# Six short loads behind the second MLP weight in a one-core decode kernel

## The chip, the core and the metric

The kernel runs on one core of a Trainium2 chip. The metric is the device time of one execution in microseconds; a kernel's time is the median of its runs. The profile that is shown comes from one execution taken by the hardware profiler; its span runs from the first to the last instruction.

## The reference, cut to what matters

One token passes through an attention branch and an MLP branch that share one normalized input. The results are added to the input.

```python
x = A_x                                   # [1, 1, 1024], bf16
xn = _layernorm(x)
return x + _A_ref(xn, k_cache, v_cache, wq, wo) + _B_ref(xn, w1, b1, w2, b2)

# attention: wq [1024, 4096], 32 query heads of 128, 4 key/value heads, last W = 4096 positions
q = (xn @ wq) ;  p = softmax(q k^T * 128**-0.5) ;  o = p v ;  return o @ wo        # wo [4096, 1024]
# MLP: w1 [1024, 3584], w2 [3584, 1024]
h = gelu(_layernorm(xn) @ w1 + b1) ;  return h @ w2 + b2
```

All weights and caches are bf16. With one token each weight is read once: wq 8.4 MB, w1 7.3 MB, w2 7.3 MB, wo 8.4 MB, and the used part of the caches 4.2 MB each, 39.85 MB together.

## The kernel before, in words

Every large operand is laid over the 128 partitions, so that each partition of a load is one contiguous run in memory (w1 and w2 are 56 KB per partition). All large loads are issued by SyncE (SP) into one DMA queue, in this order: the key cache in four loads (line 76), wq in two (line 85), w1 in one (line 200), the value cache in three (line 208), w2 in one (line 214), and wo in two halves, the first in one load and the second in five of shrinking size, 8, 4, 2, 1 and 1 rows of 1024 per partition (line 222). Four small loads go through ScalarE's queue at the start (lines 107 to 110): x as 32 partitions of 64 bytes, x and b2 as 4 partitions of 512 bytes each, b1 as 8 partitions of 896 bytes.

SP's loads are held back by the buffers that they fill. Large tiles share two slots of the pool `big` (the key cache and half of wq in one, the transposed keys in the other; later w1 takes the first and w2 the second), smaller ones two slots of `ring` (half of wq, the values, then the two halves of wo). So w1 waits until the first half of wq has been multiplied, w2 until the attention scores are done (line 260), and the second half of wo until the value product is done (line 296). The framework also gives each DMA one of eight completion semaphores in turn, and a load whose semaphore is still in use by the load eight places before it waits on SP for that load to land.

VectorE and ScalarE transpose the keys (lines 185 to 196). TensorE multiplies in the order wq (line 231), scores (260), w1 (243), values (296), w2 and wo (both line 323, into the accumulator `accf`; eight filler passes of line 321 stand between the two), and the last four rows of wo separately into `acct` (line 340). The last two steps, lines 344 and 345, add and cast the result, which goes out in two DMAs (lines 347 and 348).

The tile `w2t` has 32768 elements per partition. w2 fills 28672 of them (`CW2 * D`), the transposed activations `hT` (line 290) the next 896; the rest is unused. The list `chunk_src` holds the rows of w2 and wo that line 323 and line 340 go through.

Of the kernel before, what the change touches and what calls it, by code (L numbers as in the profile page):

```python
# [15 lines left out]
def kernel(  # L16
# [14 lines left out]
    nc = tc.nc  # L31
    P = 128
    D = A_x.shape[-1]
# [12 lines left out]
    CW2 = Fd // P  # L46
# [19 lines left out]
    def big_tile(name):  # L66
        return big.tile([P, 2 * RING_ELEMS], BF16, tag="big", name=name, align_bytes=256)
# [144 lines left out]
    w2t = big_tile("w2t")  # L212
    w2v = w2t[:, :CW2 * D].rearrange("p (r n) -> p r n", r=CW2)
    nc.sync.dma_start(out=w2v, in_=w2_v)
    chunk_src += [("h", r, w2v[:, r, :]) for r in range(CW2)]
    wo_v = A_wo.rearrange("(p c) n -> p c n", p=P)
    for i, cuts in enumerate([[0, 16], [0, 8, 12, 14, 15, 16]]):
# [8 lines left out]
    for i, w3 in enumerate(wq_tiles):  # L226
        for r in range(4):
            c = 4 * i + r
            for j in range(NJQ):
                b, t = divmod(j, 4)  # L230
# [148 lines left out]
```

## Time and profile before

| | us |
|---|---|
| median of three runs | 101.74 (101.66 to 102.03) |
| the profiled execution | 101.68 |
| its span | 100.0 |
| TensorE busy | 48.5 |
| VectorE busy | 38.2 |
| ScalarE busy | 29.2 |
| GpSimd busy | 8.6 |
| packets of SP's queue, share of 16 DMA engines over the span | 93.5% |
| moved, mean | 39.91 MB, 399 GB/s |

The time of the execution is 1.68 us above its span. Busy time of a compute engine is the time in which it executed; a share far below the span means that it waited for most of it. The DMA share is the busy time of the packets over 16 DMA engines. Besides the page's own views, the trace keeps a record of each DMA packet (queue, start, duration, size) and of each arrival at a completion semaphore; a load on all 16 DMA engines has 16 arrivals, one for each engine.

### The profile page before, as it was taken

Reading aid. Unit: us, or ns where it says so; the run is one execution under the profiler, and the core shown is the slowest. Engines: PE = TensorE matmul, PEld = TensorE weight load, DVE = VectorE, ACT = ScalarE, POOL = GpSimd, SP = SyncE. Lnnn points to the kernel's source line nnn. Section 1 sums busy time; section 2 is a strip of 40 time slices with the busy share of each in tenths; the row PEclk is TensorE's granted clock in tenths of the full one; section 3 lists DMA queues with packets and bytes.
Section 4 is the critical chain, followed back from the end, with each engine's and each line's share of the span. In section 5 each row is a group of like instructions: output and inputs, shape, how many; then the busy total and the mean of one; then the engine's idle time right before and its main releaser. Section 6 shows DMA issues by size and latency. Waiting matters only on the chain.

```text
span 100.0 us, 913 instructions
## 1 busy us (share of the span) xinstructions
PE 48.5 (49%) x361; PEld 19.5 (20%) x361; DVE 38.2 (38%) x26; ACT 29.2 (29%) x34; POOL 8.6 (9%) x33
## 2 busy tenths in 40 slices
PE   0006400008500940089149407997100999999980
PEld 0003100002100300053126203342000234224320
DVE  0069999999999970010631051002400000000020
ACT  5306100007999999900150440000400000000010
POOL 7911560000000000000001000000000000000000
PEclk9999999999995555555966997599755569999997
DMA  2999999999999888998599998998899999999910
GB/s 26 387 420 431 456 502 459 446 433 433 420 420 577 367 367 367 482 620 367 213 420 436 426 534 390 459 620 351 367 413 393 420 420 420 420 426 415 398 53 1
DMA packets 2663, 39.91 MB, mean 399 GB/s; under 512 B 338, under 2 KB 356, under 8 KB 740
## 3 DMA queue, kind: packets, MB, share of 16 engines
q1 hardware_dynamic: 2578, 39.85, 93.5%
q8 instruction: 3, 0.05, 0.2%
q10 hardware_dynamic: 82, 0.01, 0.1%
HBM read 39.86 MB, written 0.00 MB: 399 GB/s over the span
## 4 chain that ended last, share of the span: by engine, by line
DMA 80%; PE 14%; SPq 2%; issue 1%; DVE 0%
DMA v_sb<-in_A_v_cache_dram 33%; DMA wo<-in_A_wo_dram 25%; DMA kq<-in_A_wq_dram 17%; PE o_all L296 9%; DMA kq<-in_A_k_cache_dram 5%; PE accq L231 4%; SPq L222 1%; PE acct L340 1%; SPq L208 1%; DVE res L344 0%; PE acct L336 0%; SPq L200 0%
## 5 line engine op out<-in xcount | busy, mean ns | idle before, releaser
L194 ACT COPY kt<-kt 32x4096 bf16<-32x4096 bf16 x5 | 18.0, 3602 | 10.4 <-DVE kt L185 10.3
L185 DVE STREAM_TRANSPOSE kt<-kq 128x4096 bf16<-128x4096 bf16 x4 | 17.4, 4413 | 5.8 <-DMA kq<-in_A_k_cache_dram 5.8
L196 DVE COPY kt<-kt 32x4096 bf16<-32x4096 bf16 x11 | 13.4, 1219 | 0.2
L323 PE MATMUL accf<-w2t 128*1 128x512 bf16 x56 | 8.3, 466 | 5.7 <-DMA w2t<-in_B_w_dram 5.7
L296 PE MATMUL o_all<-v_sb,w1t 128*32 128x512 bf16 x32 | 8.8, 442 | 4.3 <-DMA v_sb<-in_A_v_cache_dram 4.3
L329 DVE COPY bulk<-accf 33x320 f32<-33x320 f32 x1 | 0.5, 482 | 24.7 <-ACT bulk L328 24.7
L231 PE MATMUL accq<-kq,xnT 128*1 128x512 bf16 x32 | 3.6, 627 | 10.2 <-DMA kq<-in_A_wq_dram 10.2
L323 PE MATMUL accf<-wo,o 128*1 128x512 bf16 x56 | 7.5, 378 | 0.1
L328 ACT COPY bulk<-accf 33x192 f32<-33x192 f32 x1 | 0.3, 312 | 23.2 <-PE accf L323 23.2
L231 PE MATMUL accq<-wq,xnT 128*1 128x512 bf16 x32 | 3.6, 626 | 6.1 <-DMA wq<-in_A_wq_dram 6.1
L231 PEld LDWEIGHTS <-xnT 128*1 128x1 bf16 x64 | 2.1, 116 | 20.5 <-issue 20.5
L296 PEld LDWEIGHTS <-w1t 128*32 128x32 bf16 x32 | 3.4, 109 | 9.6 <-DVE w2t L291 4.7
L323 PEld LDWEIGHTS <-w2t 128*1 128x1 bf16 x56 | 2.8, 98 | 10.8 <-issue 8.7
L243 PE MATMUL acch<-w1t,yT 128*1 128x448 bf16 x64 | 4.5, 450 | 0.0
L299 DVE TENSOR_TENSOR o_m<-o_all,grs 32x512 f32<-32x512 f32 x1 | 0.7, 678 | 9.0 <-PE o_all L296 9.0
L139 PE MATMUL x_ps<-x,zb 32*128 32x8 bf16 x4 | 0.2, 162 | 7.9 <-DMA x<-in_A_x_dram 7.9
L247 PE MATMUL qT_ps<-zb,w1t 128*128 128x128 bf16 x8 | 1.0, 311 | 6.2 <-ACT w1t L233 6.2
L303 ACT CAST o_bf<-o_f 32x128 bf16<-32x128 f32 x1 | 0.3, 297 | 12.5 <-DVE o_f L301 12.5
L291 DVE STREAM_TRANSPOSE w2t<-w1t 128x896 bf16<-128x896 bf16 x1 | 1.7, 1700 | 5.7 <-ACT w1t L288 5.7
L260 PE MATMUL sp<-kt,zb 128*32 128x512 bf16 x32 | 3.7, 631 | 0.3 <-DVE zb L252 0.3
L321 PE MATMUL spare<-zf,ident_f 128*1 128x512 f32 x8 | 3.6, 592 | 0.0
L323 PEld LDWEIGHTS <-o 128*1 128x1 bf16 x56 | 2.6, 82 | 4.3 <-issue 1.1
(78 smaller groups left out, 40.3 us busy)
## 6 DMA issues: line engine op xcount, KB each, us to landing
w1t<-in_B_w_dram SPq DMA_DIRECT2D x1, 7168.0 KB, 24.3
w2t<-in_B_w_dram SPq DMA_DIRECT2D x1, 7168.0 KB
kq<-in_A_k_cache_dram SPq DMA_DIRECT2D x4, 1024.0 KB, 8.1
kq<-in_A_wq_dram SPq DMA_DIRECT2D x1, 4096.0 KB, 17.1
wq<-in_A_wq_dram SPq DMA_DIRECT2D x1, 4096.0 KB, 24.1
wo<-in_A_wo_dram SPq DMA_DIRECT2D x1, 4096.0 KB
v_sb<-in_A_v_cache_dram SPq DMA_DIRECT2D x1, 2048.0 KB, 28.6
v_sb<-in_A_v_cache_dram SPq DMA_DIRECT2D x2, 1024.0 KB, 30.6
```

The source lines that it names most:

```text
L185: nc.vector.transpose(out=scr[:, g, :], in_=k2[:, g, :])
L194: nc.scalar.copy(out=dst, in_=src)
L196: nc.vector.tensor_copy(out=dst, in_=src)
L208: nc.sync.dma_start(out=v4[:, g0:g1, :, :], in_=src)
L222: nc.sync.dma_start(out=tv[:, a:b, :], in_=wo_v[:, nr * i + a:nr * i + b, :])
L231: nc.tensor.matmul(accq[32 * t:32 * t + 1, b, :], lhsT=xnT[:, c:c + 1], rhs=w3[:, r, j * 512:(j + 1) * 512], start=(c == 0), stop=(c == C ...
L243: nc.tensor.matmul(acch[32 * t:32 * t + 1, b, :NH], lhsT=yT[:, c:c + 1], rhs=w1v[:, c, j * NH:(j + 1) * NH], start=False, stop=(c == C - 1 ...
L260: nc.tensor.matmul(sp[32 * R:32 * R + 32, a, :], lhsT=qm[:, g, :], rhs=kT[:, g, c0:c0 + 512], start=(g == 0), stop=(g == Hkv - 1), tile_po ...
L291: nc.vector.transpose(out=hT, in_=h_sb.rearrange("p (d c) -> p c d", c=CW2))
L296: nc.tensor.matmul(o_all[:].rearrange("h g d -> h (g d)"), lhsT=eTb[:, 32 * c:32 * c + 32], rhs=v4[:, :, c, :], start=(c == 0), stop=(c == ...
L321: nc.tensor.matmul(spare[0:1, :], lhsT=ident_f[:, 0:1], rhs=zeros, start=True, stop=True)
L323: last = nc.tensor.matmul(accf[32 * half:32 * half + 1, :], lhsT=vec[kind](c), rhs=wap[:, half * 512:(half + 1) * 512], start=False, stop= ...
```

## The change

Behind the load of w2, SP issues six more loads, with 4, 4, 8, 8, 12 and 12 partitions and 5632 bytes in each. They read the first bytes of w2 again and write them into the unused end of `w2t`: load k takes partitions k, k + 8, k + 16 and so on, columns 29568 to 32383. Nothing reads what they write, and the result is computed as before. They move 48 runs of 5632 bytes, 0.27 MB.

```diff
     w2v = w2t[:, :CW2 * D].rearrange("p (r n) -> p r n", r=CW2)
     nc.sync.dma_start(out=w2v, in_=w2_v)
+    RUN = 2816
+    ramp = w2t[:, CW2 * (D + 32):CW2 * (D + 32) + RUN]
+    w2_runs = B_w2.rearrange("a b -> (a b)")
+    for k, n in enumerate((4, 4, 8, 8, 12, 12)):
+        nc.sync.dma_start(out=ramp[k:8 * n:8, :], in_=w2_runs[0:n * RUN].rearrange("(n e) -> n e", n=n))
     chunk_src += [("h", r, w2v[:, r, :]) for r in range(CW2)]
     wo_v = A_wo.rearrange("(p c) n -> p c n", p=P)
```

No instruction of TensorE, VectorE, ScalarE or GpSimd is added, removed or moved. On SP the six loads stand between the load of w2 and the first load of wo, and because the eight semaphores are given out in turn, every later load gets another one than before.

## The prediction

> **What bounds the kernel now.** I read the page's table of DMA queues first, then the windows by stage, the chain, and the end of the timeline.
>
> ```profile
> PE 48.5 (49%) x361; PEld 19.5 (20%) x361; DVE 38.2 (38%) x26; ACT 29.2 (29%) x34; POOL 8.6 (9%) x33
> ...
> q1 hardware_dynamic: 2578, 39.85, 93.5%
> q8 instruction: 3, 0.05, 0.2%
> ```
>
> No compute engine is busy for half the span, while SP's queue (q1) fills 93.5% of 16 DMA engines. The small row q8, three code fetches, matters below.
>
> ```profile
> 26.50:48.90 22.40, 8.42 (x73) 3.50 (x72) 11.63 (x12) 15.74 (x6) 0.00 (x0) 0.62 0.98 426
> 48.90:60.40 11.50, 5.11 (x69) 3.20 (x68) 3.27 (x4) 3.96 (x6) 0.53 (x2) 0.85 1.03 437
> 60.40:77.40 17.00, 9.01 (x36) 3.74 (x37) 1.68 (x2) 1.12 (x4) 0.00 (x0) 0.72 1.01 437
> 77.40:87.10 9.70, 9.66 (x60) 3.13 (x60) 0.00 (x0) 0.00 (x0) 0.00 (x0) 0.78 0.97 419
> 87.10:96.50 9.40, 9.12 (x73) 3.01 (x71) 0.48 (x1) 0.31 (x1) 0.00 (x0) 1.00 0.86 356
> ```
>
> In each row the last two numbers are the DMA share and GB/s. The share is full until 87.1 and falls to 0.86 in the last stretch: there some of the 16 engines have finished and others have not.
>
> ```profile
> 60.50 8.77 PE o_all L296 x32
> ...
> 70.58 25.00 DMA wo<-in_A_wo_dram
> 95.58 0.04 issue
> 95.62 0.60 PE acct L340 x8
> 96.22 0.42 PE acct L336 x4
> 96.64 0.56 PE acct L340 x6
> 97.20 0.02 issue
> 97.22 0.48 DVE res L344
> ```
>
> The chain ends with wo's loads and the few matmuls that wait for their last pieces. The packet records say why the end is ragged. Every DMA engine runs back to back at one fixed speed: a packet starts every 306 ns at 8192 B, 1210 ns at 32768 B, 2113 ns at 57344 B, and a completion write takes 6 ns more. The arrivals of the last load of wo are at 95.24 to 95.68 us for 14 engines, and at 96.79 and 96.84 for two. Those two lost about 1.15 us each to a code fetch of 16384 B, one at 48.80 us and one at 69.21 us (the third fetch, at 96.67, comes after the loads). Both stay late to the end. So the end is set by the later of two late engines, 1.16 us behind the last of the others, and 100.0 − 96.84 = 3.16 us of fixed work follows it.
>
> **The change part by part.**
>
> Added work on the DMA engines. Through the three packet sizes goes a line, 1807 ns / 49152 B = 0.0368 ns per byte plus 5 ns; a packet of 5632 B then takes 212 ns, with its completion write 218. The ScalarE loads check the line at small sizes: it gives 38 ns for 896 B, and the record shows the next packet 38 ns behind.
>
> Which engines get them is what decides. ScalarE's small loads show how a load of few partitions is dealt out: those of 4 partitions left one packet on each of four engines, the same four both times, and that of 8 on these four and four more. I told engines apart by the phase of their packets, which each keeps: four carry 512 B and 896 B packets (group I), four 896 B alone (group II), eight neither. The new loads should fall alike: six packets on group I, four on group II, two on four of the other eight (group III), none on the last four (group IV). At 218 ns that is 1.31, 0.87, 0.44 and 0 us. [...]
>
> These times lie on the path only where an engine is, or becomes, the last one. By its phase group I writes its last completion at 95.07 to 95.15 us; with 1.31 us that is 96.38 to 96.46. Group II ends at 95.11 to 95.35, plus 0.87 makes 95.98 to 96.22. The two late ones now write theirs at 96.468 and 96.503. So both groups stay, just, under the late engines: cost 0, with 0.04 us of cover for group I; if a packet cost a tenth more, up to 0.1 us would show.
>
> The late engines themselves: their phases before the fetches (108 and 141 ns behind the first engine) are those of engines that carried no small packet, so both are in group III or IV. Which, the trace doesn't show. With four engines in each, the chance that both are in IV is 4/8 × 3/7 = 0.21. If the later one is in III (0.50) the end moves by 0.44; if only the earlier is (0.29), by 96.468 + 0.436 − 96.503 = 0.40. I take 0.43.
>
> Does the compute behind it follow one to one? wo's first half lands at 87.06 and would at 87.50; TensorE is in its filler passes until 88.5, so that start is covered. Its first wait in the stream is for the second piece of the second half, which lands at 94.35 and lets the last weight loads start at 94.39; pieces three to five are waited for at 95.58, 96.20 and 96.84. All of these move with the late engine, so the tail moves whole: one to one.
>
> SP. Six issues at 0.33 to 0.47 us (its rows for lines 214 and 208) are about 2.7 us of SP's time, and in the compiled queue some now wait for the landing of earlier loads through the semaphores given in turn: the fourth for w1 (50.80), the fifth and sixth for the first two pieces of values (55.51, 57.94), wo's first load for the third (60.37), wo's second half for w2 (77.39) in place of line 296 (69.27). Behind these stand only wo's loads and, 20 us later, the output. The queue runs dry at 75.4 without wo's first half, so that issue at 60.4 in place of 48.0 has some 14 us to spare; without the second half it runs dry at 85.4, so that issues from 77.4 to about 79.7 (five at 0.45) have over 5 us. Cost 0; the cover would be gone if the second half were issued after about 84.
>
> TensorE's order is unchanged, so I keep the code fetches where they are and on the same engines. Bounds for the whole: below, 0, since no byte, wait or instruction on the path is removed; above, the 1.31 us of group I in full, if a late engine belonged to it.
>
> Sum: 101.68 + 0.43 = 102.11 for the profiled execution, which stands 0.06 below the median; against the median 102.17. I write 102.15, 0.4% over. Of this kernel about 0.5% (0.5 us) can be told from no change.
>
> **The rivals.**
>
> *Hidden altogether.* Both late engines are in group IV: end unchanged, 101.7 to 101.85. For it: 0.21 by count; against it: nothing but the count.
>
> *Code fetches fall elsewhere.* If the fetches hit other engines in other executions or with another program, a late engine can be in group I or II, and its 1.15 us adds to the 1.31 or 0.87: group I would end at 96.46 + 1.15 = 97.61, +1.1 us; group II at 96.22 + 1.15, +0.9. Time 102.6 to 102.9, slower. It decides as soon as one of the two is in these groups. For it: one trace can't show that the place is fixed. Against it: TensorE's code, whose steps the fetch times match (48.80 is the restart at line 265, 69.21 the end of line 296), is unchanged.
>
> [...]
>
> *A short load holds the queue.* If each of the six held its engine for more than its bytes, say for the 1.0 us between the first issue and the first packet at the start of the kernel, group I would be 6 us late and the time 106 to 107. Against it: in the records the next packet starts 6 ns behind a completion write, at every one of the queue's 17 loads. [...] The trace doesn't bear it out as time of the engine: ScalarE's 2 KB loads delayed the stream by 24 ns a packet.
>
> *Faster.* I find no mechanism; 0.04 is left for one that I don't see.
>
> **How the numbers follow.** Late engine in III: 0.50 (+0.40 to +0.46, with about 0.1 us for landing and measurement: three in ten of it measured over 0.5%). Hidden: 0.20. Fetches elsewhere: 0.12. Shared partitions: 0.12, three quarters of it over 0.5%. Queue held: 0.02. Faster: 0.04. Slower by over 0.5%: 0.15 + 0.12 + 0.09 + 0.02 = 0.38; within 0.5%: 0.35 + 0.20 + 0.03 = 0.58; faster: 0.04. The range goes from the hidden case, 101.6, to the fetch case, 102.9; the likeliest case alone spans 102.0 to 102.3.
>
> **What would show it.** In the changed kernel's records: packets of 5632 B 212 ns apart, 48 of them, right behind w2 at 75.4 to 76.9; twelve engines that carry six, four or two of them; arrivals of the last wo load in steps; a last arrival near 97.25. A last arrival at 96.84 means that the late engines carried none. Packets well over 212 ns, or ordinary packets slower beside them, speak for shared partitions; a late engine with four or six packets for the fetch rival. SP's issues of wo near 60.4 and 77.4 to 80. I would be wrong if the queue ran dry before wo, or if the 5632 B packets were not dealt out in nested groups.

## The result and the profile after

The changed kernel takes 103.26 us (median of six runs, 102.75 to 103.36) against 101.73 before: the ratio is 1.0136 with a 95% interval of 1.0111 to 1.0160, slower by 1.4%. The forecast was 102.15 and its range ended at 102.9. The ratios here leave out executions more than 1.5% above the fastest of their kernel; where a kernel has many of those, its median stands above its ratio.

The page's table of queues after the change:

```profile
q1 hardware_dynamic: 2674, 40.12, 93.7%
q8 instruction: 3, 0.05, 0.2%
```

96 packets and 0.27 MB more in SP's queue: 48 runs and 48 completion writes. The three code fetches are still there. The end of the chain:

```profile
79.16 17.84 DMA wo<-in_A_wo_dram
97.00 0.04 issue
97.04 0.60 PE acct L345 x8
97.64 0.42 PE acct L341 x4
98.06 0.57 PE acct L345 x6
98.63 0.02 issue
98.65 0.48 DVE res L349
```

It has the same shape, 1.43 us later: the last matmuls and the result wait for wo's last pieces, whose last arrival is at 98.27 us in place of 96.84. So the whole difference stands in the DMA stream. SP's own timeline shows that it isn't a late issue:

```profile
46.70 0.33 SPq L214 DMA_DIRECT2D w2t<-in_B_w_dram  x1
47.08 11.52 SPq L219 DMA_DIRECT2D w2t<-in_B_w_dram  x6
60.29 20.25 SPq L227 DMA_DIRECT2D wo<-in_A_wo_dram  x6
```

wo's first load is issued at 60.29 and the last at about 80, long before the queue reaches them. The windows by stage of the changed kernel, those that answer to the last three shown of before:

```profile
60.40:77.40 17.00, 10.11 (x36) 4.03 (x37) 2.02 (x3) 1.12 (x4) 0.00 (x0) 0.70 1.04 424
77.40:87.10 9.70, 8.82 (x57) 3.02 (x57) 0.00 (x0) 0.00 (x0) 0.00 (x0) 0.70 0.95 401
87.10:96.50 9.40, 9.07 (x64) 2.88 (x62) 0.00 (x0) 0.00 (x0) 0.00 (x0) 1.00 0.96 403
```

The 437 and 419 GB/s of before have become 424 and 401, and up to 96.5 the engines are still full (0.96 in place of 0.86). Where the time goes shows closer in the window in which the six loads run. First the kernel before, then the changed one; the last two numbers are the DMA share and GB/s:

```profile
75.40:79.40 4.00, 1.97 (x10) 0.60 (x11) 0.00 (x0) 0.00 (x0) 0.00 (x0) 0.50 1.16 500
79.40:88.00 8.60, 8.60 (x55) 2.69 (x52) 0.00 (x0) 0.00 (x0) 0.00 (x0) 0.87 0.93 400
```

```profile
75.40:79.40 4.00, 1.12 (x6) 0.35 (x7) 0.00 (x0) 0.00 (x0) 0.00 (x0) 0.50 1.10 361
79.40:88.00 8.60, 8.60 (x55) 2.84 (x52) 0.00 (x0) 0.00 (x0) 0.00 (x0) 0.78 0.95 410
```

The engines are nearly as busy as before, but move 361 GB/s in place of 500. The view counts a packet whole in the window in which it starts, so that short windows swing: 500 stands above the 437 of the long windows. Counted from the packet records by the part of each packet that lies in the window, it is 319 GB/s in place of 433. Behind it the rate is normal again (410, before 400; by parts of packets 433 both times). The packet records of that stretch (a record lasts 3 ns longer than the time to the next packet's start, so the 212 ns of the forecast stand as 215):

| | before | changed |
|---|---|---|
| 5632 B packets, the first 16 (75.38 to 75.74 us) | | 215 ns each |
| the other 32 | | 265 to 489 ns |
| first wo packet (32768 B), the 14 engines that are not late | 1213 ns | 1622 to 1985 ns |
| last w2 packet (57344 B) of the two late engines | 2116 ns | 2714 and 2853 ns |
| wo packets over 1221 ns, their time above 1213 ns in all | 0 | 25, 11.7 us |

The two late engines carry two of the new packets each (from 77.43 and from 77.54 us), so they are in group III. All four groups are slowed: the four engines that carry none (group IV) take 1651 to 1702 ns for their first wo packet. For the last of them the sum closes: its last w2 packet takes 0.737 us longer, its two new packets with their completion writes 0.681, its first wo packet 0.176, the second 0.006, together 1.60; its last w2 packet began 0.174 earlier than that of the last engine before (74.680 against 74.854). That leaves 1.43 us, which is what the last arrival moved. Of the 1.60 the forecast had 0.44.

### The profile page after: what moved, and what is told of

Its sections match the earlier page's. It is cut to its first block, busy times and chain, and to the rows that moved or that the text cites. A ratio compares the mean times of both kernels' runs of the same rounds, so it can differ in the third digit from the quotient of the medians.

```text
span 101.5 us, 917 instructions
## 1 busy us (share of the span) xinstructions
PE 50.1 (49%) x361; PEld 20.4 (20%) x361; DVE 38.2 (38%) x26; ACT 29.2 (29%) x34; POOL 8.6 (8%) x33
## 4 chain that ended last, share of the span: by engine, by line
DMA 77%; ACT 12%; PE 6%; SPq 1%; DVE 1%; issue 1%; DVEq 0%
DMA w2t<-in_B_w_dram 31%; DMA wq<-in_A_wq_dram 22%; DMA wo<-in_A_wo_dram 18%; ACT kt L194 11%; DMA kq<-in_A_k_cache_dram 7%; PE sp L265 3%; PE acct L345 1%; PE qT_ps L252 1%; ACT w1t L238 1%; SPq L227 1%; DVE res L349 0%; PE acct L341 0%; SPq L76 0%; DVE zb L257 0%; SPq L214 0%
## 5 line engine op out<-in xcount | busy, mean ns | idle before, releaser
L301 PE MATMUL o_all<-v_sb,w1t 128*32 128x512 bf16 x32 | 9.9, 484 | 3.8 <-DMA v_sb<-in_A_v_cache_dram 3.8
L248 PE MATMUL acch<-w1t,yT 128*1 128x448 bf16 x64 | 5.7, 535 | 0.0
L296 DVE STREAM_TRANSPOSE w2t<-w1t 128x896 bf16<-128x896 bf16 x1 | 1.7, 1702 | 6.8 <-ACT w1t L293 6.8
L248 PEld LDWEIGHTS <-yT 128*1 128x1 bf16 x64 | 3.5, 118 | 1.8
```

Source lines behind the costliest of these rows:

```text
L248: nc.tensor.matmul(acch[32 * t:32 * t + 1, b, :NH], lhsT=yT[:, c:c + 1], rhs=w1v[:, c, j * NH:(j + 1) * NH], start=False, stop=(c == C - 1 ...
L296: nc.vector.transpose(out=hT, in_=h_sb.rearrange("p (d c) -> p c d", c=CW2))
L301: nc.tensor.matmul(o_all[:].rearrange("h g d -> h (g d)"), lhsT=eTb[:, 32 * c:32 * c + 32], rhs=v4[:, :, c, :], start=(c == 0), stop=(c == ...
```

## The experiments

**What is slow: the place read or the place written?** Two readings of the traces stood against each other. Theory D: the loads write to partitions that other engines write to. Theory S: up to 12 engines read one small piece of w2, six times over. In the first run each partition reads the start of its own row block:

```diff
+    w2_rows = B_w2.rearrange("(p c) n -> p (c n)", p=P)
-        nc.sync.dma_start(out=ramp[k:8 * n:8, :], in_=w2_runs[0:n * RUN].rearrange("(n e) -> n e", n=n))
+        nc.sync.dma_start(out=ramp[k:8 * n:8, :], in_=w2_rows[k:8 * n:8, 0:RUN])
```

> The six loads as in the change, to the same partitions and columns, but each partition reads the start of its own row block of w2 (57344 B apart per partition) instead of all six loads reading the same first 67 KB of w2. Theory D (the loads slow the streams because engines write to partitions that other engines write to): the destinations are unchanged, so about 103.2 us as in the change (+1.5), 5632 B packets up to 300 to 490 ns, group IV's first wo packet near 1.65 us. Theory S (one small piece of HBM, read by up to 12 engines at once and six times over, is the bottleneck): packets back at 212 to 215 ns, group IV's wo packets at 1213 ns, the late engines only two packets later, 102.1 to 102.2 us (+0.4).

Measured: 102.94 us, ratio 1.0121 (1.0078 to 1.0164). The window:

```profile
75.40:79.40 4.00, 1.05 (x6) 0.35 (x7) 0.00 (x0) 0.00 (x0) 0.00 (x0) 0.50 1.11 402
```

29 of the 48 packets are slow, that is more than 8 ns over their undisturbed time (up to 372 ns), and 23 wo packets take up to 1889 ns. The slowing has not gone, so theory S falls for the most part. The profiled execution (102.74 us) shows one more thing: its two late engines carry none of the new packets, and yet the last arrival is at 97.75, 0.91 us later than before, since their last w2 packets take 2874 and 3015 ns. A late engine without a packet of its own pays for those of others.

The second run gives each load its own piece of w2:

```diff
-        nc.sync.dma_start(out=ramp[k:8 * n:8, :], in_=w2_runs[0:n * RUN].rearrange("(n e) -> n e", n=n))
+        s0 = 12 * k * RUN
+        nc.sync.dma_start(out=ramp[k:8 * n:8, :], in_=w2_runs[s0:s0 + n * RUN].rearrange("(n e) -> n e", n=n))
```

> The six loads as in the change, but load k reads its own 67 KB of w2 (offset 12 x k x 5632 B), so that no byte is read twice, while the runs of one load still lie behind one another. Theory D: 103.2 us. Theory S in the form 'the same bytes six times over': about 102.2 us. Theory S in the form 'engines read runs that lie close together': 102.6 to 103.2 us.

Measured: 103.32 us, ratio 1.0174 (1.0117 to 1.0231), 33 slow packets, 24 slow wo packets. Reading the same bytes again is not the cause.

**The step between partitions.** Two kernels with loads of 4, 4, 8, 8, 8, 8 partitions from the same source. One keeps the step of 8:

```diff
-    for k, n in enumerate((4, 4, 8, 8, 12, 12)):
+    for k, n in enumerate((4, 4, 8, 8, 8, 8)):
```

> Loads of 4, 4, 8, 8, 8, 8 partitions (the two loads of 12 cut to 8), partitions k + 8i as in the change, same source; the late engines carry no packet now. By the packet price alone the end is unchanged, 101.7 to 101.8 us (group I ends 0.04 us before the late engines). Theory D: group I and II engines slowed, and others only where they share partitions, 102.0 to 102.8. Theory S: every stream slowed, the late engines by some 0.8 to 1.1 us, 102.5 to 102.9 us. It is the partner of the run with steps of 4 partitions.

The other goes in steps of 4:

```diff
-    for k, n in enumerate((4, 4, 8, 8, 12, 12)):
-        nc.sync.dma_start(out=ramp[k:8 * n:8, :], in_=w2_runs[0:n * RUN].rearrange("(n e) -> n e", n=n))
+    for k, n in enumerate((4, 4, 8, 8, 8, 8)):
+        p0 = k if k < 4 else 32 + k - 4
+        nc.sync.dma_start(out=ramp[p0:p0 + 4 * n:4, :], in_=w2_runs[0:n * RUN].rearrange("(n e) -> n e", n=n))
```

> [...] Theory S: within 0.2 us of the partner with steps of 8.

Measured: step 8 ran at 102.56 to 104.41 us, ratio 1.0154 (1.0065 to 1.0243); step 4 at a median of 102.01, ratio 1.0043 (1.0019 to 1.0068). The windows, step 8 first:

```profile
75.40:79.40 4.00, 0.69 (x4) 0.21 (x5) 0.00 (x0) 0.00 (x0) 0.00 (x0) 0.50 1.11 376
```

```profile
75.40:79.40 4.00, 1.76 (x10) 0.58 (x11) 0.00 (x0) 0.00 (x0) 0.00 (x0) 0.50 1.12 478
```

With step 8, 26 of 40 packets and 40 wo packets are slow. With step 4 all 40 packets take 215 ns, all 128 wo packets 1213 ns, and the engines that carry six and four of them end 1.3 and 0.9 us later, by the price of the forecast, still ahead of the late ones. The same bytes from the same place through the same number of packets cost nothing beyond that price when they go to other partitions. So it is the place written that counts. Theory D's reason for it, engines that write to the same partitions, stays the author's reading: no record shows which partitions an engine writes in the large loads. The times alone would not settle it: those of step 8 scatter, and its interval begins inside that of step 4. The packet records rule theory S out. The trace of step 8 is of an execution of 104.2 us; the step-8 runs below show the same slowing in executions of 102.6 and 102.8 us.

The 102.01 us of step 4 stand above the 101.7 to 101.8 that the packet price alone gave. In its trace the last arrival is at 97.02, 0.18 us later than before, but the two engines that end late already start w2 0.19 and 0.22 us later than those of before, some 15 us ahead of the new loads.

The pair also tells of the late engines. The profiled execution with step 8 (104.2 us) has a late engine that carries four packets (its w2 ends at 77.93, its packets start at 77.94, 78.23, 78.45 and 78.70, wo at 79.08): group II. So the code fetches don't always hit engines of groups III and IV. The ten times with step 4 fall into seven at 101.82 to 102.08 and three at 102.61 to 102.84; the three would fit a late engine with four packets (+0.87), which is argued, since no trace of it shows one.

**How far does it spread, and is it the step itself?** Four loads of 8 partitions, all on groups I and II, once in steps of 8 from partition 0 and once in steps of 4 from partition 4. Theory G takes it that an engine has partitions of its own in the large loads; that is the author's assumption, shown by no record.

```diff
-    for k, n in enumerate((4, 4, 8, 8, 12, 12)):
-        nc.sync.dma_start(out=ramp[k:8 * n:8, :], in_=w2_runs[0:n * RUN].rearrange("(n e) -> n e", n=n))
+    for k in range(4):
+        nc.sync.dma_start(out=ramp[k:64:8, :], in_=w2_runs[0:8 * RUN].rearrange("(n e) -> n e", n=8))
```

> Four loads of 8 partitions at k + 8i, all on the eight engines of groups I and II, 32 packets of 5632 B. Partner of the next run. [...] Theory G (a write outside an engine's own partitions that has to wait holds up all streams): wo's first packets on all 16 engines at 1.5 to 1.9 us, as in the change. [...]

```diff
-        nc.sync.dma_start(out=ramp[k:64:8, :], in_=w2_runs[0:8 * RUN].rearrange("(n e) -> n e", n=8))
+        nc.sync.dma_start(out=ramp[4 + k:4 + k + 29:4, :], in_=w2_runs[0:8 * RUN].rearrange("(n e) -> n e", n=8))
```

> [...] Theory G in the form that any write outside an engine's own partitions slows the streams: like the partner with steps of 8.

Measured: step 8 took 102.60 to 105.17 us in three runs, too scattered for a ratio; the rotated one 101.99, ratio 1.0020 (1.0009 to 1.0031). Step 8 first, then the rotated one:

```profile
75.40:79.40 4.00, 1.25 (x8) 0.37 (x9) 0.00 (x0) 0.00 (x0) 0.00 (x0) 0.50 0.98 356
```

```profile
75.40:79.40 4.00, 1.97 (x10) 0.61 (x11) 0.00 (x0) 0.00 (x0) 0.00 (x0) 0.50 1.14 487
```

In the rotated run all 32 packets stay at 215 ns, no wo packet is slow, and the last arrival is at 96.83 us, where it was before (96.84). It is not like its partner, so theory G in its wide form finds no support here. In steps of 8 the eight engines that carry no packet are slowed too: the six of them that are not late take 1699 to 1852 ns for their first wo packet in place of 1213, and the two late ones 2859 and 2925 for their last w2 packet in place of 2116. So what it costs depends on the partitions written, and engines that write none of the new packets pay too.

Loads of 4 partitions alone, all between partitions 0 and 29:

```diff
-    for k, n in enumerate((4, 4, 8, 8, 12, 12)):
-        nc.sync.dma_start(out=ramp[k:8 * n:8, :], in_=w2_runs[0:n * RUN].rearrange("(n e) -> n e", n=n))
+    for k in range(6):
+        nc.sync.dma_start(out=ramp[k:32:8, :], in_=w2_runs[0:4 * RUN].rearrange("(n e) -> n e", n=4))
```

> Six loads of 4 partitions at k + 8i, 24 packets, six on each of the four engines of group I and none elsewhere. [...] Theory G: all streams slowed, though by less than in the change with half the packets, 102.0 to 102.6 us.

Measured: ratio 1.0097 (1.0077 to 1.0118), 102.73 us in the fastest run. 26 wo packets are slow, and the ten engines that carry nothing and are not late take 1768 to 1868 ns for their first. That is a little above the 102.0 to 102.6 of theory G. With half the packets of the change the last arrival moves by 0.94 us (to 97.78), as far as the 0.91 with the spread source, where the late engines carry nothing either.

The step of 8 could itself be what is slow. The next run has the same number of loads of 4 in steps of 4, placed at partitions 16 to 31 and 48 to 61:

```diff
-        nc.sync.dma_start(out=ramp[k:32:8, :], in_=w2_runs[0:4 * RUN].rearrange("(n e) -> n e", n=4))
+        p0 = 16 + k if k < 4 else 48 + k - 4
+        nc.sync.dma_start(out=ramp[p0:p0 + 13:4, :], in_=w2_runs[0:4 * RUN].rearrange("(n e) -> n e", n=4))
```

> Six loads of 4 partitions again, 24 packets on the four engines of group I, but in steps of 4: partitions 16 + 4i + k (four loads) and 48 + 4i + k (two). [...] Theory K (the step of 8 partitions itself is what is slow): free as the two other runs with steps of 4, packets at 215 ns, wo packets at 1213 ns, 101.75 to 101.85 us.

Measured: 105.02 us, ratio 1.0294 (1.0262 to 1.0325), the slowest of all. The window of the loads and the next one:

```profile
75.40:79.40 4.00, 0.84 (x6) 0.25 (x7) 0.00 (x0) 0.00 (x0) 0.00 (x0) 0.50 1.18 378
79.40:88.00 8.60, 8.60 (x58) 2.94 (x55) 0.00 (x0) 0.00 (x0) 0.00 (x0) 0.81 0.95 366
```

Theory K is out: with a step of 4 at these partitions all is slowed as with 8 (the first wo packets take 1475 to 1951 ns). It went further than expected: the rate doesn't recover behind the loads (366 GB/s against the changed kernel's 410 in the same window).

**The price of the bytes, and of half of them.** One load over all partitions with the same 0.27 MB:

```diff
-    RUN = 2816
+    RUN = 1056
+    w2_rows = B_w2.rearrange("(p c) n -> p (c n)", p=P)
-    for k, n in enumerate((4, 4, 8, 8, 12, 12)):
-        nc.sync.dma_start(out=ramp[k:8 * n:8, :], in_=w2_runs[0:n * RUN].rearrange("(n e) -> n e", n=n))
+    nc.sync.dma_start(out=ramp, in_=w2_rows[:, 0:RUN])
```

> One load of 128 partitions with 2112 B in each, 0.27 MB as in the change, in place of the six: each engine gets the same eight packets on its own partitions. By the packet line 8 x (0.0368 x 2112 + 5) + 6 = 667 ns on every engine, the late ones too, whichever they are: 102.4 us (+0.67) by all theories. If bytes alone cost more than the line says, it is above; it prices the bytes without the way they are dealt out.

Measured: 102.37 us against 101.74, +0.63, ratio 1.0063 (1.0041 to 1.0084). The packet price holds. The same bytes dealt out by the six loads cost 1.5 us.

The change with packets of half the size:

```diff
-    RUN = 2816
+    RUN = 1408
```

> The change with half the bytes in each packet, 2816 B (0.135 MB in all). In the change the first 16 packets or so, some 85 KB, ran at full speed and the slowing began 0.45 us behind the first one. If that much is always taken in without delay, a quarter of the slowing is left: 0.27 x 1.0 + 0.23 us for the packets of the late engines, 102.2 us. If the slowing goes with the bytes: half of it, 102.45 us. If a packet's conflict costs the same whatever its size: 103.0 us.

Measured: 102.51 us against 101.79, ratio 1.0078 (1.0061 to 1.0095). 43 of the 48 packets run at full speed (112 ns; the others take 114 to 198), but 14 wo packets behind them are slow (1422 to 1580 ns) and the late engines' last w2 packets take 2474 and 2572 ns. Those two carry none of the new packets in this trace, and the last arrival is at 97.39, 0.55 us later than before, against 0.91 in the trace with the spread source, where they carry none either. In time it is 0.72 against 1.5 us. With the same six loads half the bytes give about half the delay or a little more. Bytes alone don't set it, though: the six loads of 4 partitions move the same 0.135 MB and moved the last arrival by 0.94 in place of 0.55. And that the first packets run at full speed doesn't make them free; the delay shows on the packets behind them.

## Why the prediction was wrong

What bounds the kernel was right: the last arrival moved by 1.43 us, the end of the chain by the same, and the profiled execution by 1.58 (101.68 to 103.26), the rest of which lies outside the span or in its last steps.

The packet price was right where no ordinary packet was slow: in the two free runs (step 4 and the rotated one) all 72 packets of 5632 B last 215 ns in the records, 212 from start to start as the line gave, and +0.63 against 0.67 for the bytes over all engines. That the loads fall in nested groups of 4, 8 and 12 engines was right, and so was the likeliest case, a later late engine in group III, in the profiled execution. SP's issues were where they were forecast, 60.3 and 78 to 80 us, and cost nothing.

The step that failed is the sum for the late engine: "If the later one is in III (0.50) the end moves by 0.44". The forecast was +0.43 us, and +1.53 were measured. The sum took the packets at their undisturbed speed and ordinary packets beside them as untouched. The runs put 1.60 us in the place of 0.44: 0.74 for the ordinary w2 packet in flight, 0.68 for the two new packets, 0.18 for the next two. So the term that it put at nothing, the delay of packets beside and of the new packets themselves, was 1.16 us. The cover of 0.04 us for group I was no issue, and "Hidden altogether" would not have held either: with late engines that carry nothing, the run with a spread source still moved its last arrival by 0.91 us.

What came was nearest to the forecast's "Shared partitions", which had a chance of 0.12, and its sign had been named: packets well over 212 ns and ordinary packets slower beside them. No run shows that term as such, engines that share partitions; the runs showed in its place that packets of the same number and size from the same source are free or slow by the partitions that they go to, and that engines without a new packet are held up as well. ScalarE's small loads at the start, 11 KB, had left no mark on the phases beyond their own packets; but the first 16 packets of the change, 90 KB, kept their 215 ns too, and the delay fell on the packets behind them. A row that shows no effect at a 25th of the size doesn't exclude one.

"I keep the code fetches where they are and on the same engines" was not safe: the second fetch came at 71.15 us in place of 69.21 in the changed kernel's trace, and the trace of the first step-8 run has a late engine in group II. In the changed kernel's own trace it held by group.

The size of a code fetch was read wrong too. The prediction says that the two engines "lost about 1.15 us each", but 1.16 us is the distance to the last of the others. In the trace of before, the fetch at 69.21 us holds up its engine's next packet by 0.95 us, and that packet takes 2585 ns in place of 2116: 1.42 us together. The sum for the late engine doesn't use this figure, but the rival "Code fetches fall elsewhere" does: with 1.42 its groups would have ended some 0.27 us later, and its time would have been 102.9 to 103.1 us.

That the partitions written decide it is shown: step 4 against step 8 (no packet slow, against 26 of 40 and 40 wo packets), the rotated run against its partner (no slow wo packet, against first wo packets of 1699 to 1852 ns on engines that carry none of the new packets). That it is two engines writing to one place was the author's estimate and isn't shown, and neither is the way by which the delay reaches the other engines.

## What to carry to other kernels

Price a short load by where it writes, not by its bytes alone: the same 0.27 MB cost 0.63 us as one load over all partitions and 1.5 us as the six. In these runs a load of 4 to 12 partitions ran on as many engines. At partitions in steps of 8 from 0, and in steps of 4 from 16 and 48, all streams slowed (first wo packets of 1475 to 1985 ns in place of 1213), and in one run they stayed slow (366 GB/s against 410). In steps of 4 from partitions 0 and 32, and from 4, the loads cost only their packets, 215 ns each. In a kernel bound by its DMA stream read the arrivals engine by engine: here the end was set by the last engine (before, 1.16 us behind the last of the 14 others that were not late), and the average share, 0.86 from 87.1 to 96.5 us, doesn't show which one that is.

## What was not expected of the hardware

A few packets on four engines slow the others: six loads of 4 partitions in steps of 8, 0.135 MB, raised the first wo packet on the ten engines that carry nothing and aren't late from 1213 to 1768 ns and more.

In the run of fours in steps of 4 the slowing outlived the loads by some 20 us. The last 5632 B packet ended at 77.5, but all 128 wo packets of 32768 B stayed at 1359 ns or more, and packets of 8192 B took 342 ns in place of 309 up to 96.7. In the changed kernel the wo packets were back at 1213 ns by 80 us. What keeps the streams slow there, and why only there, was not tried.

A code fetch of 16 KB, 0.88 to 0.96 us in the records where it falls into the stream, made its engine about 1.42 us late for the rest of the kernel in the trace of before (next packet 0.95 us later, and 2585 ns long in place of 2116), and which engines are hit differs from trace to trace: groups III and III in the changed kernel, IV and IV with the spread source, one in II with step 8.
